# Block-diagonal state and one-chunk pipelining in linear attention, full-width stationary operands in a Fourier layer

## The chip, the cores and the metric

The kernel runs on one core of a Trainium2 chip. The metric is the device time of one execution in microseconds (us). Profile times below are counted from the first instruction of the profiled execution.

## The reference

Two layers follow each other. The first is linear attention with a decay per head: batch 4, 8 heads, 768 positions, head size 64. The second is a Fourier mixing layer on the joined heads (model size 512) with an MLP of inner size 2048. All data is fp32.

```python
for b in range(nb):                      # blocks of the sequence
    intra = (q_b @ k_b.T * Dmask) @ v_b  # Dmask = lam ** (i - j) for i >= j
    inter = (q_b * lam_pow) @ kv_state   # kv_state: 64 x 64 per head
    out[:, :, sl] = intra + inter
    kv_state = lam_block * kv_state + (k_b * rev_pow).T @ v_b
...
x = out.transpose(0, 2, 1, 3).reshape(B, S, H * D)
u = x + real(fft(fft(x, axis=1), axis=2))
un = (u - mean(u)) / sqrt(var(u) + 1e-06)
return u + relu(un @ w_ch1) @ w_ch2
```

The result does not depend on the block size, and the kernel uses chunks of 128 positions, so there are six chunks per batch.

## The kernel before

**Stages.** The program is written as Python generators that yield estimated costs; a hand-written weave (`beside`, `weave`, `part`, at the end of the kernel) takes turns between them, and a scheduler at build time may still move an instruction of an engine ahead of another unless it is pinned with `tc.keep_in_program_order`. Each engine then runs its own list strictly in order. The weave first runs attention of batch 0 beside the conversion of weights, then the Fourier layer of batch 0 beside attention of batch 1, then, from about 95 us on, the MLP of the first four groups of rows with everything else of the front end (attention and Fourier of batches 1 to 3) woven into it. From about 430 us on the MLP of the remaining rows runs alone (`late`), with products that the change does not touch.

**Attention, one chunk.** `attn_in` (L259) loads k, q and v on SP's queue (two buffers each), multiplies k by its decay on GpSimd (L270, tile kd, one buffer), transposes k and q on TensorE (L274, L279) and copies both out of PSUM on ScalarE (L276, L281). The 8 heads stand as 4 pairs: head 2p is on partitions 0 to 63 and head 2p+1 on 64 to 127 of pair p. From the transposed q VectorE also makes qs, q times its decay (L285). `attn_out` (L289) makes the scores (L298), one product per head with 64 rows and 128 columns of the array, masks them on VectorE (L302, tile sc), makes the state update (L315, 128 rows and 64 columns), and adds to the output in PSUM first the state product (L328, 64 rows and 64 columns, st times qs) and then the masked scores times v (L332, 128 rows and 64 columns). The state has two tiles that take turns: GpSimd multiplies the old one by the decay of a chunk (L319), VectorE adds the update (L320), and the state product of the chunk reads the old one. The output is copied by ScalarE (L335), transposed back (L348) and copied out (L352, L353). For batches other than 0, rows go to DRAM and are gathered back mirrored by GpSimd's queue (`mirror_a`, `mirror_b`, L439 to L452) for the Fourier layer.

In each group of eight products the two heads of a pair follow each other, so that the two halves of the array take turns. PSUM tiles of attention and Fourier layer share five buffers (`psum_a`).

**Fourier layer.** `fft_ln` (L491) folds rows with their mirror images on VectorE (`fold_x`, L426 to L484), transforms along the sequence with five products per batch, each of two output parts and two pieces of rows (L516), copies the results on ScalarE (L520), and transforms along the width (`width`, L524, matmuls L529 to L534). The fifth product of the sequence step needs one output row, and so does a last call of `width` (`only_a`, L607): both use a stationary operand of one column. Then `norm` (L542) takes mean and variance on VectorE, the root on GpSimd (L550, L551), and normalises (L564).

**Weights** come as 512 KB pieces on SP's queue (L209) and each is converted by two steps on ScalarE and five on VectorE (L216 to L225).

Of the kernel before, what the change touches and what calls it, by code (L numbers as in the profile page):

```python
# [10 lines left out]
F32 = mybir.dt.float32  # L11
# [65 lines left out]
def kernel(  # L77
# [95 lines left out]
    mhalf = const.tile([128, G], F32, name="mhalf")  # L173
    nc.gpsimd.memset(mhalf, -0.5)

    st = [const.tile([128, HP, D], F32, name=f"st{i}") for i in range(2)]


    cs = const.tile([128, 2, 2, 2, NK], F32, name="cs")
# [65 lines left out]

    def attn(b):

        head = () if b - 1 in LEADS else attn_in(b, 0)
        for c in range(NC):
            yield from head  # L250
            head = attn_in(b, c + 1) if c < NC - 1 else attn_in(b + 1, 0) if b in LEADS else ()
            yield from attn_out(b, c, head)

    ins, oTs, eo = {}, {}, {}
    LEADS = (0,)
# [3 lines left out]
    def attn_in(b, c):  # L259
        rows = slice(c * C, (c + 1) * C)  # L260
        kt, qt, vt = (new(ld, [C, H, D], nm) for nm in ("k", "q", "v"))
        for t, src in ((kt, k), (qt, q), (vt, v)):
            nc.sync.dma_start(t, src[b, :, rows, :].rearrange("h p d -> p h d"))
        if b == 0:
            load_tables(c)

        kd = None
        if c < NC - 1:
            kd = new(at, [C, H, D], "kd")
            nc.gpsimd.tensor_tensor(kd, kt, kpow, op=ALU.mult)  # L270

        ptk = psum_a([128, HP, C])
        for hp in range(HP):
            nc.tensor.transpose(ptk[:, hp, :], pair(kt, hp), ident)  # L274
        kT = new(at, [128, HP, C], "kT", bufs=2)
        nc.scalar.copy(kT, ptk)  # L276
        ptq = psum_a([128, HP, C])
        for hp in range(HP):
            nc.tensor.transpose(ptq[:, hp, :], pair(qt, hp), ident)  # L279
        qT = new(at, [128, HP, C], "qT", bufs=2)  # L280
        nc.scalar.copy(qT, ptq)  # L281
        qs = None
        if c > 0:
            qs = new(at, [128, HP, C], "qs")
            nc.vector.tensor_tensor(qs, ptq, qpow, op=ALU.mult)  # L285
        ins[b, c] = kT, qT, qs, kd, vt
        yield 1.2

    def attn_out(b, c, head):  # L289
        kT, qT, qs, kd, vt = ins.pop((b, c))  # L290
        last = c == NC - 1


        mm = nc.tensor.matmul
        pss = [psum_a([C, HP, C]) for _ in range(2)]
        for hp in range(HP):
            for hi in range(2):
                mm(pss[hi][:, hp, :], lhsT=kT[HD[hi], hp, :], rhs=qT[HD[hi], hp, :], start=True, stop=True)  # L298
        sc = []
        for hi in range(2):  # L300
            t = new(at, [C, HP, C], "sc", bufs=3)
            nc.vector.tensor_tensor(t, pss[hi], decay[:, hi::2, :], op=ALU.mult)  # L302
            sc.append(t)
        if last and b - 1 in LEADS:
            mirror_a(b, pin=True)
        yield 1.5


        s_old, s_new = st[(c + 1) % 2], st[c % 2]
        if not last:  # L310
            pu = psum_a([128, HP, D])
            for hp in range(HP):
                for hi in range(2):
                    h = 2 * hp + hi
                    mm(pu[HD[hi], hp, :], lhsT=kd[:, h, :], rhs=vt[:, h, :], start=True, stop=True)  # L315
            if c == 0:
                nc.vector.tensor_copy(s_new, pu)
            else:
                nc.gpsimd.tensor_tensor(s_new, s_old, spow.broadcast_to([128, HP, D]), op=ALU.mult)  # L319
                nc.vector.tensor_tensor(s_new, s_new, pu, op=ALU.add)  # L320
            yield 0.9


        po = psum_a([128, HP, C])
        if c > 0:
            for hp in range(HP):
                for hi in range(2):
                    mm(po[HD[hi], hp, :], lhsT=s_old[HD[hi], hp, :], rhs=qs[HD[hi], hp, :],  # L328
                       start=(hp == 0), stop=False, skip_group_check=True)
        for hp in range(HP):  # L330
            for hi in range(2):
                mm(po[HD[hi], hp, :], lhsT=vt[:, 2 * hp + hi, :], rhs=sc[hi][:, hp, :],  # L332
                   start=(c == 0 and hp == 0), stop=(hp == HP - 1), skip_group_check=True)
        oT = new(at, [128, HP, C], "oT")
        nc.scalar.copy(oT, po)  # L335
# [6 lines left out]
        yield 2.0  # L342
        yield from head

        def turn(oT):
            px = psum_a([C, HP, 128])
            for hp in range(HP):
                nc.tensor.transpose(px[:, hp, :], oT[:, hp, :], ident)  # L348
# [36 lines left out]

        px = turn(oTs[b]) if c > 1 else None
        if c > 0:

            oTs[b] = new(fp, [128, DM + 4], "ds")[:, 0:DM].rearrange("p (h c) -> p h c", h=HP)
            tc.keep_in_program_order(nc.scalar.copy(oTs[b][:, :, C - 1:0:-1], po[:, :, 1:C]))  # L390
        if last:
            tc.keep_in_program_order(nc.scalar.copy(oTs[b][:, :, 0:1], first))
        if c > 1:
            mirrored(c - 1, px)
            yield 1.4
        if not last:
# [94 lines left out]
    def fft_ln(b):  # L491
        sets = []

        def piece(a, i, n):

            c0 = W + QM if i == 4 else QM * (i % 2)
            return sets[a][i in (2, 3)][0:BLK[a], n, c0:c0 + (1 if i == 4 else QM)]

        if b in LEADS:
            yield from fold_a(b)  # L500
# [10 lines left out]
        for i in range(5):  # L511
            ps = psum_a([128, 2, NK])
            m = 128 if i < 4 else 1
            for n in range(2):
                for a, rows in enumerate(BLK):
                    mm = nc.tensor.matmul(ps[0:m, n, :], lhsT=piece(a, i, n), rhs=cs[0:rows, a, i in (2, 3), n, :],  # L516
                                          start=(a == 0), stop=(a == 1))
                    if i + n + a == 0:
                        tc.keep_in_program_order(mm)
            nc.scalar.copy(ys[i][0:m, 0:2 * NK].rearrange("p (k n) -> p n k", n=2), ps[0:m])  # L520
            yield 1.4


        def width(t, ps, only_a):  # L524
            y = [ys[i][:, 128 * t:min(128 * t + 128, S // 2 + 1)] for i in range(5)]
            ps = ps[0:1] if only_a else ps
            mm = nc.tensor.matmul
            if not only_a:
                mm(ps[:, HM + QM:DM], lhsT=y[2], rhs=dt[:, 2, 0:QM], start=True, stop=True)  # L529
# [651 lines left out]
    def run(gen):  # L1181
        return sum(gen)
# [20 lines left out]

    att1, mix = attn(1), fft_ln(0)
    att0 = attn(0)
    run(part(att0, 2.7))
    run(beside(att0, NC * t_chunk - 2.7, w, 0.25 * NW))

    run(beside(part(mix, T_FOLD), T_FOLD, att1, 3.25 * t_chunk))
# [55 lines left out]
```

## Time and profile before

| | us |
|---|---|
| median of 3 runs (799.5 to 799.83) | 799.71 |
| the profiled execution's own time | 799.14 |
| its span, first to last instruction | 797.2 |
| TensorE matmuls busy | 768.7 (96%) |
| VectorE busy | 586.4 (74%) |
| ScalarE busy | 217.3 (27%) |
| GpSimd busy | 196.5 (25%) |

The page's chain that ended last lies to 79% on TensorE. In lines of the profile, `128*64 128x128` behind a matmul is the part of the array that the stationary operand takes (rows*columns) and the operand that is streamed (partitions x elements). An fp32 product counts as two passes, so eight products are `x16`; a transpose counts as one. PEld is the load of the stationary operand. A busy matmul includes the end of its pipeline, so how long a group holds TensorE is read from the start of one group to the start of the next.

### The profile page before, as it was taken

How to read it: one execution, taken by the hardware profiler on the slowest of the kernel's cores; microseconds unless marked ns; L12 is line 12 of the kernel's file. 1: busy time of each engine (PE TensorE's matmuls, PEld its weight loads, DVE VectorE, ACT ScalarE, POOL GpSimd, SP SyncE). 2: the span in 40 equal slices, each digit the busy share in tenths (PEclk: the TensorE clock that was granted, in tenths of full speed). 3: DMA queues.
4: the chain of work that ended last, by engine and by line, in shares of the span. 5: the costliest groups of instructions: out<-in, count | busy, mean ns of one | idle time of the engine just before them, and what ended most of it. 6: DMA issues, size and time to landing. Idle time of an engine off the chain costs nothing.

```text
span 797.2 us, 14576 instructions
## 1 busy us (share of the span) xinstructions
PE 768.7 (96%) x5616; PEld 643.0 (81%) x5616; DVE 586.4 (74%) x1148; ACT 217.3 (27%) x512; POOL 196.5 (25%) x196
## 2 busy tenths in 40 slices
PE   6989999999999999999999999999999999999996
PEld 5767766758575766777855889998999999999996
DVE  6898889775844573246597998669977699758983
ACT  3755443224421211221200221012210342024300
POOL 3233340011111020121002960279304100230012
PEclk9999999999999999999999999999999999999998
DMA  9969623237842136443232365345854555455442
GB/s 252 253 148 271 181 84 121 81 75 202 215 122 83 40 66 141 101 136 107 49 67 83 145 234 168 103 159 193 318 176 145 163 183 175 131 173 183 135 120 80
DMA packets 152331, 116.80 MB, mean 147 GB/s; under 512 B 113998, under 2 KB 113998, under 8 KB 152262
## 3 DMA queue, kind: packets, MB, share of 16 engines
q1 hardware_dynamic: 147120, 103.39, 45.7%
q0 software_dynamic: 2112, 6.69, 2.6%
q10 hardware_dynamic: 3030, 5.78, 2.1%
q8 instruction: 45, 0.74, 0.4%
q14 instruction: 24, 0.20, 0.1%
HBM read 83.58 MB, written 32.25 MB: 145 GB/s over the span
## 4 chain that ended last, share of the span: by engine, by line
PE 79%; DVE 9%; DMA 4%; issue 4%; ACT 2%; POOL 1%; POOLq 0%; ACTq 0%; DVEq 0%
PE p L1038 21%; PE p L883 12%; PE p L968 11%; PE pm L650 10%; PE pm L636 8%; PE pa L332 3%; PE pa L516 3%; PE pa L298 3%; DMA x<-xb,ix 2%; PE pa L328 2%; PE pa L274 1%; PE pa L315 1%; DVE sc L302 1%; PE pa L279 1%; PE pa L348 1%
## 5 line engine op out<-in xcount | busy, mean ns | idle before, releaser
L636 PE MATMUL pm<-ut,w 128*128 128x256 f32 x512 | 119.2, 382 | 0.0
L650 PE MATMUL pm<-w,hr 128*128 128x512 f32 x256 | 116.1, 598 | 0.2 <-DVE w L225 0.2
L636 PEld LDWEIGHTS pm<-ut,w 128*128 128x128 f32 x512 | 94.4, 190 | 15.4 <-issue 3.6
L650 PEld LDWEIGHTS pm<-w,hr 128*128 128x128 f32 x256 | 46.9, 191 | 49.8 <-issue 48.2
L1052 POOL TENSOR_TENSOR y<-y,u 128x512 f32<-128x512 f32 x12 | 18.9, 1572 | 199.1 <-DVE y L1061 156.7
L1038 PE MATMUL p<-tx,sx 128*128 128x128 f32 x416 | 54.9, 275 | 0.0
L1038 PEld LDWEIGHTS p<-tx,sx 128*128 128x128 f32 x416 | 50.6, 192 | 0.0
L883 PE MATMUL p<-ur,w 128*128 128x256 f32 x192 | 46.9, 379 | 0.1
L270 POOL TENSOR_TENSOR kd<-k,decay 128x512 f32<-128x512 f32 x20 | 23.0, 1152 | 93.8 <-PE pa L315 60.7
L1046 DVE TENSOR_TENSOR y<-p,y 128x128 f32<-128x128 f32 x92 | 25.6, 286 | 22.4 <-PE p L1038 15.7
L1044 ACT COPY y<-p 128x128 f32<-128x128 f32 x48 | 12.8, 266 | 104.1 <-PE p L1038 103.8
L883 PEld LDWEIGHTS p<-ur,w 128*128 128x128 f32 x192 | 36.3, 190 | 5.7 <-issue 0.5
L302 DVE TENSOR_TENSOR sc<-pa,decay 128x512 f32<-128x512 f32 x48 | 31.5, 683 | 8.4 <-PE pa L298 8.2
L1038 PE MATMUL p<-w,ha 128*128 128x128 f32 x288 | 37.4, 275 | 0.0
L298 PEld LDWEIGHTS pa<-qT,kT 64*128 64x128 f32 x384 | 26.0, 193 | 13.1 <-ACT qT L281 7.2
L332 PE MATMUL pa<-sc,v 128*64 128x128 f32 x384 | 32.3, 286 | 3.5 <-DVE sc L302 3.5
L1038 PEld LDWEIGHTS p<-w,ha 128*128 128x128 f32 x288 | 35.0, 192 | 0.2
L644 ACT ACTIVATE hr<-pm 128x256 f32<-128x256 f32 x44 | 16.7, 385 | 67.5 <-PE pm L636 67.3
L550 POOL TENSOR_SCALAR ve<-mv 128x2 f32<-128x2 f32 x12 | 3.4, 287 | 123.3 <-DVE mv L547 123.3
L298 PE MATMUL pa<-qT,kT 64*128 64x128 f32 x384 | 30.7, 292 | 3.2 <-ACT qT L281 2.9
L883 PE MATMUL p<-sx,w1s 128*128 128x256 f32 x128 | 32.9, 380 | 0.2 <-DVE sx L786 0.2
L332 PEld LDWEIGHTS pa<-sc,v 128*64 128x64 f32 x384 | 23.6, 139 | 11.2 <-DVE sc L302 5.3
(227 smaller groups left out, 1709.0 us busy)
## 6 DMA issues: line engine op xcount, KB each, us to landing
tx<-td SPq DMA_DIRECT2D x84, 256.0 KB, 2.8
raw<-in_moe_w_ch_dram SPq DMA_DIRECT2D x32, 512.0 KB, 5.3
tx<-sd SPq DMA_DIRECT2D x42, 256.0 KB, 2.7
sd<-tx SPq DMA_DIRECT2D x28, 256.0 KB, 2.0
k<-in_k_dram SPq DMA_DIRECT2D x24, 256.0 KB, 5.0
q<-in_q_dram SPq DMA_DIRECT2D x24, 256.0 KB, 5.7
v<-in_v_dram SPq DMA_DIRECT2D x24, 256.0 KB, 4.8
td<-tx SPq DMA_DIRECT2D x21, 256.0 KB, 2.0
```

What stands on the lines that cost most here:

```text
L270: nc.gpsimd.tensor_tensor(kd, kt, kpow, op=ALU.mult)
L298: mm(pss[hi][:, hp, :], lhsT=kT[HD[hi], hp, :], rhs=qT[HD[hi], hp, :], start=True, stop=True)
L302: nc.vector.tensor_tensor(t, pss[hi], decay[:, hi::2, :], op=ALU.mult)
L332: mm(po[HD[hi], hp, :], lhsT=vt[:, 2 * hp + hi, :], rhs=sc[hi][:, hp, :], start=(c == 0 and hp == 0), stop=(hp == HP - 1), skip_group_chec ...
L516: mm = nc.tensor.matmul(ps[0:m, n, :], lhsT=piece(a, i, n), rhs=cs[0:rows, a, i in (2, 3), n, :], start=(a == 0), stop=(a == 1))
L636: nc.tensor.matmul(ps, lhsT=w1[:, c, 128 * fc:128 * fc + 128], rhs=ut[:, c, :], start=(c == 0), stop=(c == KO - 1))
L650: nc.tensor.matmul(ps, lhsT=hr[(fc - f0) // 4][:, fc % 4, 128 * i:128 * i + 128], rhs=w2[:, fc, :], start=(fc == f0), stop=(fc == f1 - 1))
L883: nc.tensor.matmul(ps, lhsT=s2.A[a][:, kt, 128 * i:128 * i + 128], rhs=U[b][:, kt, :], start=(first and kt == 0), stop=(kt == 1), skip_gro ...
L968: nc.tensor.matmul(ps[:, 128 * i:128 * i + 128], lhsT=ab[m][0][:, 128 * i:128 * i + 128], rhs=ab[m][1], start=(start and i == 0), stop=Tru ...
L1038: nc.tensor.matmul(ps[:, 0:HM // 2], lhsT=ab[m][0][i], rhs=ab[m][1][:, i, :], start=(start and i == 0), stop=(i == HF // 2 - 1), skip_grou ...
L1046: V.tensor_tensor(o, ps[:, 0:HM // 2], o, op=ADD)
L1052: nc.gpsimd.tensor_tensor(o, y, u, op=ADD)
```

## The change

The state becomes one tile of 128 partitions with, for each pair of heads, two blocks of 64 columns: block 0 holds head 2p on partitions 0 to 63 and zeros below, block 1 zeros and then head 2p+1. The tile is cleared once on GpSimd. The state product then uses all 128 rows of the array and 64 columns, as the output product and the state update do. The decay of a chunk (L318 of the new program) runs in place on the whole tile, and the add of the update (L324) runs once for each half of the partitions.

Attention is reordered: scores and mask of chunk c+1 (`attn_first`) are issued ahead of the state product of chunk c; qs of the next chunk is made after the state product, from the copied q in SBUF instead of PSUM; state product, output product and state update follow each other in this order, the first instruction of each pinned. Masked scores get four buffers for three, the transposed k one for two. `attn` starts the next chunk's input ahead of the transposes of the last chunk's output.

In the Fourier layer the fifth product of the sequence step takes 128 columns and writes 128 rows of PSUM, of which the copy still reads one; the last call of `width` streams against one column repeated 128 times.

```diff
-    st = [const.tile([128, HP, D], F32, name=f"st{i}") for i in range(2)]
+    st = const.tile([128, HP, 2, D], F32, name="st")
+    nc.gpsimd.memset(st, 0.0)
...
     def attn(b):
-        head = () if b - 1 in LEADS else attn_in(b, 0)
+        if b - 1 not in LEADS:
+            yield from attn_in(b, 0)
+            attn_first(b, 0)
+        back = ()
         for c in range(NC):
-            yield from head
-            head = attn_in(b, c + 1) if c < NC - 1 else attn_in(b + 1, 0) if b in LEADS else ()
-            yield from attn_out(b, c, head)
+            nxt = (b, c + 1) if c < NC - 1 else (b + 1, 0) if b in LEADS else None
+            if nxt:
+                yield from attn_in(*nxt)
+            yield from back
+            back = attn_out(b, c, nxt)
+            yield from part(back, 4.4)
+        yield from back
...
-        kT = new(at, [128, HP, C], "kT", bufs=2)
+        kT = new(at, [128, HP, C], "kT")
...
-        qs = None
-        if c > 0:
-            qs = new(at, [128, HP, C], "qs")
-            nc.vector.tensor_tensor(qs, ptq, qpow, op=ALU.mult)
-        ins[b, c] = kT, qT, qs, kd, vt
+        ins[b, c] = kT, qT, kd, vt
...
+    def attn_state(b, c):
+        kd, vt = ins[b, c][2:]
+        pu = psum_a([128, HP, D])
+        for hp in range(HP):
+            for hi in range(2):
+                h = 2 * hp + hi
+                mm = nc.tensor.matmul(pu[HD[hi], hp, :], lhsT=kd[:, h, :], rhs=vt[:, h, :], start=True, stop=True)
+                if h == 0:
+                    pin(mm)
+        if c > 0:
+            nc.gpsimd.tensor_tensor(st, st, spow.broadcast_to([128, HP, 2 * D]).rearrange("p h (a d) -> p h a d", a=2), op=ALU.mult)
+        for hi in range(2):
+            s = st[HD[hi], :, hi, :]
+            if c == 0:
+                nc.vector.tensor_copy(s, pu[HD[hi]])
+            else:
+                nc.vector.tensor_tensor(s, s, pu[HD[hi]], op=ALU.add)
...
+        if nxt:
+            if nxt[1]:
+                attn_first(*nxt)
         if last and b - 1 in LEADS:
             mirror_a(b, pin=True)
...
-                    mm(po[HD[hi], hp, :], lhsT=s_old[HD[hi], hp, :], rhs=qs[HD[hi], hp, :],
-                       start=(hp == 0), stop=False, skip_group_check=True)
+                    i = mm(po[HD[hi], hp, :], lhsT=st[:, hp, hi, :], rhs=qs[:, hp, :],
+                           start=(hp == 0), stop=False, skip_group_check=True)
+                    if hp + hi == 0:
+                        pin(i)
...
+        if not last:
+            attn_state(b, c)
+        if nxt and nxt[1] == 0:
+            attn_first(*nxt)
+        elif nxt:
+            qs = scores[(*nxt, 1)] = new(at, [128, HP, C], "qs")
+            nc.vector.tensor_tensor(qs, ins[nxt][1], qpow, op=ALU.mult)
...
-            return sets[a][i in (2, 3)][0:BLK[a], n, c0:c0 + (1 if i == 4 else QM)]
+            return sets[a][i in (2, 3)][0:BLK[a], n, c0:c0 + QM]
...
-                    mm = nc.tensor.matmul(ps[0:m, n, :], lhsT=piece(a, i, n), rhs=cs[0:rows, a, i in (2, 3), n, :],
+                    mm = nc.tensor.matmul(ps[:, n, :], lhsT=piece(a, i, n), rhs=cs[0:rows, a, i in (2, 3), n, :],
...
-            y = [ys[i][:, 128 * t:min(128 * t + 128, S // 2 + 1)] for i in range(5)]
-            ps = ps[0:1] if only_a else ps
+            y = [ys[i][:, S // 2:S // 2 + 1].broadcast_to([128, 128]) if only_a else ys[i][:, 128 * t:128 * t + 128] for i in range(5)]
...
-    run(part(att0, 2.7))
+    run(part(att0, 1.3))
```

`attn_first(b, c)` holds the scores and their mask as they stood in `attn_out` (L295 to L303), and keeps the masked scores in a table by chunk.

More of the change, by code (lines that the diff above doesn't have):

```diff
@@ L281, in attn_in, with attn_first @@
         nc.scalar.copy(qT, ptq)
-        qs = None
-        if c > 0:
-            qs = new(at, [128, HP, C], "qs")
-            nc.vector.tensor_tensor(qs, ptq, qpow, op=ALU.mult)
-        ins[b, c] = kT, qT, qs, kd, vt
+        ins[b, c] = kT, qT, kd, vt
         yield 1.2
[L289 to L294, printed above, removed]
+    scores, pin = {}, tc.keep_in_program_order
+    def attn_first(b, c):
+        kT, qT = ins[b, c][:2]
         pss = [psum_a([C, HP, C]) for _ in range(2)]
@@ L297, in attn_out @@
             for hi in range(2):
-                mm(pss[hi][:, hp, :], lhsT=kT[HD[hi], hp, :], rhs=qT[HD[hi], hp, :], start=True, stop=True)
-        sc = []
+                nc.tensor.matmul(pss[hi][:, hp, :], lhsT=kT[HD[hi], hp, :], rhs=qT[HD[hi], hp, :], start=True, stop=True)
+        sc = scores[b, c] = []
         for hi in range(2):
-            t = new(at, [C, HP, C], "sc", bufs=3)
+            t = new(at, [C, HP, C], "sc", bufs=4)
             nc.vector.tensor_tensor(t, pss[hi], decay[:, hi::2, :], op=ALU.mult)
@@ L304, in attn_out @@
+    def attn_out(b, c, nxt):
+        last = c == NC - 1
+        mm = nc.tensor.matmul
+        if nxt:
+            if nxt[1]:
+                attn_first(*nxt)
         if last and b - 1 in LEADS:
             mirror_a(b, pin=True)
[L306 to L311, printed above, removed]
+        sc, vt = scores.pop((b, c)), ins[b, c][3]
+        po = psum_a([128, HP, C])
+        if c > 0:
+            qs = scores.pop((b, c, 1))
@@ L312, in attn_out @@
             for hp in range(HP):
                 for hi in range(2):
[L314 to L328, printed above, removed]
-                       start=(hp == 0), stop=False, skip_group_check=True)
+                    i = mm(po[HD[hi], hp, :], lhsT=st[:, hp, hi, :], rhs=qs[:, hp, :],
+                           start=(hp == 0), stop=False, skip_group_check=True)
+                    if hp + hi == 0:
+                        pin(i)
         for hp in range(HP):
@@ L331, in attn_out @@
             for hi in range(2):
-                mm(po[HD[hi], hp, :], lhsT=vt[:, 2 * hp + hi, :], rhs=sc[hi][:, hp, :],
-                   start=(c == 0 and hp == 0), stop=(hp == HP - 1), skip_group_check=True)
+                i = mm(po[HD[hi], hp, :], lhsT=vt[:, 2 * hp + hi, :], rhs=sc[hi][:, hp, :],
+                       start=(c == 0 and hp == 0), stop=(hp == HP - 1), skip_group_check=True)
+                if hp + hi == 0:
+                    pin(i)
+        if not last:
+            attn_state(b, c)
@@ L341, in attn_out @@
                 nc.scalar.copy(oTs[b][:, :, 0:1], po[:, :, 0:1])
-        yield 2.0
-        yield from head
+        ins.pop((b, c))
+        yield 4.4
         def turn(oT):
```

## The prediction

> **What bounds the kernel now.** First the page's shares (96% TensorE), then the busy time stage by stage, then TensorE's waits, then the timeline of single groups. In the table by stretch the columns are start:end and length, then busy us and count of TensorE, its weight loads, VectorE, ScalarE and GpSimd, then TensorE clock, DMA share and GB/s.
>
> ```profile
> 0.00:50.00 50.00, 40.36 (x450) 32.26 (x450) 39.86 (x81) 29.95 (x66) 13.43 (x25) 1.00 0.95 236
> 50.00:100.00 50.00, 45.68 (x505) 38.06 (x504) 43.93 (x95) 24.13 (x55) 18.21 (x16) 1.00 0.78 205
> 126.00:210.00 84.00, 82.87 (x503) 59.23 (x502) 61.66 (x133) 33.49 (x72) 8.11 (x12) 1.00 0.55 145
> 210.00:265.00 55.00, 53.93 (x327) 35.98 (x326) 27.48 (x59) 12.71 (x27) 9.05 (x9) 1.00 0.38 103
> 300.00:366.00 66.00, 66.00 (x497) 46.76 (x496) 22.17 (x45) 12.72 (x30) 11.59 (x13) 1.00 0.56 139
> ```
>
> There are two regimes. From about 100 us, attention is woven into the MLP's products and TensorE is never free (66.00 of 66): any TensorE time removed there shortens the kernel. Before 100 us, attention of batches 0 and 1 stands with the conversion of weights and the Fourier step of batch 0; VectorE is 88% busy between 50 and 100 us, the DMA engines 95% before 50 us, and TensorE itself idles 14 us. Time saved on TensorE there may just become waiting.
>
> What TensorE waits for before 50 us, then between 50 and 100 us (total, times, longest):
>
> ```profile
> PE pa L274 <- DMA k<-in_k_dram: 4.8, 1, 4.8
> PE pa L298 <- ACT qT L281: 1.9, 4, 0.7
> PE pa L332 <- DVE sc L302: 1.1, 2, 1.0
> ```
> ```profile
> PE pa L348 <- ACT oT L335: 1.2, 1, 1.2
> PE pa L328 <- DVE qs L285: 0.8, 1, 0.8
> ```
>
> Short waits on the chain scores, mask, output. Now one chunk in the second regime (start, length, group; a product counts as two passes, so x16 is eight products):
>
> ```profile
> 203.18 2.74 PE L650 MATMUL pm<-w,hr 128*128 128x512 f32 x6
> 205.85 1.16 PE L298 MATMUL pa<-qT,kT 64*128 64x128 f32 x16
> 206.95 3.70 PE L650 MATMUL pm<-w,hr 128*128 128x512 f32 x8
> 210.58 0.69 PE L315 MATMUL pa<-v,kd 128*64 128x64 f32 x16
> 211.19 1.09 PE L328 MATMUL pa<-qs,st 64*64 64x128 f32 x16
> 212.21 1.09 PE L332 MATMUL pa<-sc,v 128*64 128x128 f32 x16
> 213.24 0.66 PE L274 MATMUL pa<-ident,k 128*128 128x128 f32 x4
> 213.73 0.60 PE L279 MATMUL pa<-ident,q 128*128 128x128 f32 x4
> ```
>
> Take distances from start to start. A dense 512-column pass takes 0.43 us (8 passes of L650 ahead of an untiled group take 3.43), so a 128-column pass 0.107. L298, L328 and L332 alternate between two halves of the array that run at once: 16 passes need 16 x 0.107 / 2 = 0.86 us, those of L315 (64 columns) 0.43. They take 1.10, 1.02, 1.03 and 0.61. So each group pays 0.16 to 0.24 us when its tiling ends, whoever follows. Entering costs too: the x6 group takes 2.67 where 2.58 is due (+0.09 into 64*128), the x8 group 3.63 where 3.43 is due (+0.2 into 128*64). The first transposes after a tiled group take 0.49, plain ones 0.44 (+0.05).
>
> [...] 1-column and 128-column products of the width step both take 0.22 us a pair. [...] the state's decay on GpSimd (L319), 0.62 at its shortest, once took 3.82 us.
>
> **The change, part by part.** I count in the order of TensorE's instructions, before and as the changed program is built, and split at the first MLP product (about 95 us).
>
> *Block-diagonal state, pinned groups.* The state product becomes 128*64 like the output product, and state product, output product and state update run as one group. Behind the split the order before has 34 runs of L315, L328 or L332 that end in another tiling, the new one 12: 22 x 0.17 = 3.7 us. Entries from untiled work into such a run fall from 14 to 2: 12 x 0.19 = 2.3. Returns to untiled work fall from 33 to 14: 19 x 0.05 = 0.9. Ahead of the split: ends 34 to 12 (3.7) and entries 5 to 2 (0.6). This presumes that state product to output product to update, one tiling but different operands, costs nothing between them. The trace does not show that junction; it lies between 0 and the 0.17 of an ended group. I take 0, because the width products change operands and lengths within one tiling at 0.22 a pair with nothing extra. The product itself keeps 128 streamed columns, so 0.86 us; zeros cost nothing more.
>
> *Alternation.* In four of the 24 score groups the old order puts two or three products on the same half in a row; they took 1.51 to 1.66 us where others take 1.10. In the new order all 24 alternate: 4 x 0.48 = 1.9 us, half of it behind the split.
>
> *Fourier products.* The fifth height product (one column) and the last width group (one column) are tilings of their own: behind the split seven runs at 0.09 in and 0.09 out, 7 x 0.18 = 1.3 us, one run (0.2) ahead. With 128 columns the products last as long as their neighbours (L516: 0.16 a pass either way), so nothing is added. More PSUM rows are written, but ScalarE still copies one.
>
> *Pipelining.* Scores and mask of chunk c+1 now precede the outputs of chunk c. That takes the mask (L302) off TensorE's path. In exchange, input transposes of chunk c+2 stand right behind the state update of chunk c. No instruction is added on TensorE.
>
> *Added on VectorE.* The state add is split by halves: two of about 0.41 (0.33 start to start) for one of 0.41, 20 chunks: 20 x 0.33 = 6.6 us, of which 10 x 0.33 = 3.3 ahead of the split. The scaled queries now read SBUF for PSUM, 0.68 either way[...]. Behind the split VectorE is 34 to 73% busy in the stretches shown, so its share hides there behind MLP products; without that cover it would be 3.3 us.
>
> *Added on GpSimd.* The decay covers 128x512 for 128x256: L270, the same size, takes 1.06, so +0.44 on 0.62, 16 times, 7 us on an engine busy 25%. It is issued before the next kd multiply (L270), waits for the state product and has finished about when the update group ends (1.3 us later), so it costs nothing unless blocked. The clearing of the state at the start (128x512, an estimate of 0.5 from the 0.42 of a 128x386 one) ends before k lands at 4.76: nothing.
>
> *Queues.* On SP the first two chunks' k, q and v now come ahead of tables and weights, so each weight is loaded about one place later and one fewer is converted before the first normalisation (-2.5 us of VectorE there). Every moved load keeps its two buffers. The pinned gather for batch 1 stands on GpSimd ahead of the first normalisation's root; three gathers at 1.0 to 1.2 each can hold that root back some 3 us.
>
> *Sum.* Behind the split 3.7 + 2.3 + 0.9 + 0.9 + 1.3 = 9.1. Two waits there should move by about a microsecond each way (an L516 wait of 1.23 near 370 gains MLP cover; chunks back to back near 330 to 350 may wait for k): net 0. Ahead of the split TensorE sheds 3.7 + 0.6 + 1.0 + 0.2 = 5.5, but VectorE sets the end: it idles some 11 us in waits between 8 and 100 us, takes on 3.3, sheds 2.5, and the root may be late. Bounds: -3 to +5.5; I take 1.5. What is late next there is VectorE's Fourier chain. Together 10.6: span 797.2 - 10.6 = 786.6. The profiled execution took 799.14 for a span of 797.2, so 1.9 lies outside: 788.5; the median of the runs is 0.6 above that execution: 789.1.
>
> **Rivals.** *Loads of k come late.* A buffer of k is free after the kd multiply of the chunk (1.06 behind the update group); k takes 5.0 us to land. It was then needed about two chunks later, now one: 1.1 + 0.4 issue + 5.0 = 6.5 us, against 5.7 for a back-to-back chunk of the new order. At 0.7 a chunk for some 11 such chunks 7.7 us are lost: 796.8. For it: DMA at 95% before 50 us. Against it: the loop covers two chunks, and TensorE waits for k once only now.
>
> [...] Then the junctions keep 0.17 each, some 38 in all, 6.3 lost: 795.4. For it: the junction isn't shown. Against it: the width products.
>
> *The state's chain takes over: slower.* The state product waits for decay and two adds of the chunk before; with it in a pinned group everything in TensorE's queue waits, MLP products too. Its cover shrinks from the 6 us of a chunk to 2.8 (transposes and scores between). If decay is blocked as at 72.50 (3.82 us) and the adds stand behind three weight steps (1.9 us on VectorE), the state is ready 2.5 + 1.9 + 0.8 = 5.2 us after the update, 2.4 late. It decides from 0.66 us a chunk over 16 chunks, the whole gain; at 1 us each 16 are lost: 794.5 if only a third are so, 805.1 if all. For it: VectorE at 88%. Against it: median decay is 0.67, and behind 210 us VectorE is half idle.
>
> **How the numbers follow.** Forecast 0.62 (its own times 784 to 793), late k 0.15[...], state chain 0.08, the rest, early stage better than bounded or the root's delay larger, 0.07. The range 784 to 797 takes in the sum with all 5.5 early microseconds and one wait gone, and both milder rivals. Faster by over 0.2% (what a measurement of this kernel can tell from no change: below 798.1) 0.88, within 0.04, slower 0.08.
>
> **What would show it.** Right: state product, output product and update start 0.86, 0.86 and 0.6 us apart, no score group over 1.2, no one-column group, fewer TensorE us between 126 and 366. Wrong: 1.02 still between state and output product; TensorE waiting for k or for the state in each early chunk; the first MLP product no earlier than now, or later.

## The result, and the profile after

The changed kernel takes 810.06 us (median of 7 runs, 807.67 to 810.61), the kernel before 799.83 in the same series: ratio 1.0111, 95% interval 1.0086 to 1.0135. It is slower, by 10.2 us between the medians, 8.9 by the ratio. The forecast was 789.1 (784 to 797).

The profiled execution took 810.3 us for a span of 808.4 (before: 799.14 and 797.2). First the same stretches of time as before, in the changed kernel (start:end and length, busy us and count of TensorE, its weight loads, VectorE, ScalarE and GpSimd, then TensorE clock, DMA share and GB/s):

```profile
0.00:50.00 50.00, 34.17 (x386) 29.76 (x388) 38.11 (x72) 24.32 (x51) 13.87 (x25) 0.90 0.85 213
50.00:100.00 50.00, 42.74 (x530) 38.48 (x526) 47.58 (x92) 25.47 (x62) 14.23 (x11) 0.97 0.72 180
100.00:126.00 26.00, 18.92 (x100) 16.51 (x101) 17.13 (x43) 8.96 (x24) 5.25 (x7) 0.87 0.31 97
...
300.00:366.00 66.00, 65.42 (x512) 46.92 (x511) 32.65 (x66) 13.21 (x29) 11.87 (x13) 1.00 0.49 107
```

Two things stand out. In the first 50 us TensorE is busy 34.17 us where it was 40.36, and part of that at a granted clock of 0.90 in the mean where it was 1.00. And VectorE is now busy 47.58 of the 50 us that follow, where it was 43.93. From 300 to 366 us TensorE is full in both kernels (65.42 and 66.00).

What TensorE waits for before 50 us, then from 50 to 100 us:

```profile
PE pa L282 <- DMA k<-in_k_dram: 7.6, 3, 5.0
PE pa L301 <- ACT qT L289: 3.8, 5, 1.0
PE pa L371 <- DVE st L324: 1.8, 1, 1.8
PE pa L287 <- DMA q<-in_q_dram: 1.2, 1, 1.2
```
```profile
PE pa L301 <- ACT qT L289: 2.9, 4, 1.4
PE pa L340 <- DVE qs L356: 1.4, 1, 1.4
```

Before, only the first k was waited for (4.8; it is the 5.0 of the 7.6 here). Now one chunk behind the split, to be laid beside the chunk shown of before (start, length, group):

```profile
344.57 1.16 PE L301 MATMUL pa<-qT,kT 64*128 64x128 f32 x16
345.66 1.09 PE L340 MATMUL pa<-qs,st 128*64 128x128 f32 x16
346.59 1.04 PE L346 MATMUL pa<-sc,v 128*64 128x128 f32 x16
347.46 0.64 PE L314 MATMUL pa<-v,kd 128*64 128x64 f32 x16
348.03 0.66 PE L282 MATMUL pa<-ident,k 128*128 128x128 f32 x4
```

Start to start: scores 1.09, state product 0.93 (was 1.02), output product 0.87 (was 1.03), update with its exit 0.57. The state product and the output product no longer pay an end of tiling, as forecast (0.93 and 0.87 for 1.02 and 1.03); the junction between them, and the zeros in the state, cost 0.07 at most (0.93 for the 0.86 due).

So where did the time go? The first MLP product starts at 110.57 us instead of 95.50: 15.1 us are lost ahead of the split. From there to the first product of the last stage it takes 330.3 us instead of 334.0: 3.7 us are won. Together 11.4, the difference of the spans (11.2) to within 0.2.

### The profile page after: what moved, and what is told of

The parts are those of the page before. It is cut to its first block, busy times and chain, and to the rows that moved or that the text cites. A ratio compares the mean times of both kernels' runs of the same rounds, so it can differ in the third digit from the quotient of the medians.

```text
span 808.4 us, 14623 instructions
## 1 busy us (share of the span) xinstructions
PE 759.5 (94%) x5616; PEld 650.7 (80%) x5616; DVE 606.5 (75%) x1168; ACT 217.3 (27%) x512; POOL 196.4 (24%) x197
## 4 chain that ended last, share of the span: by engine, by line
PE 71%; DVE 15%; issue 5%; DMA 3%; ACT 2%; POOL 2%; SPq 1%; POOLq 0%; ACTq 0%; DVEq 0%
PE p L1060 21%; PE p L905 12%; PE p L990 11%; PE pm L672 9%; PE pm L658 6%; PE pa L539 3%; PE pa L301 2%; PE pa L340 2%; PE pa L346 1%; DVE un L586 1%; DVE sc L305 1%; DVE stt L568 1%; DVE w L226 1%; POOL rs L573 1%; DMA x<-xb,ix 1%
## 5 line engine op out<-in xcount | busy, mean ns | idle before, releaser
L318 POOL TENSOR_TENSOR st<-st,qpow 128x512 f32<-128x512 f32 x16 | 19.6, 1226 | 109.3 <-PE pa L340 76.9
L664 DVE TENSOR_SCALAR hr<-pm 128x256 f32<-128x256 f32 x20 | 8.4, 418 | 32.5 <-PE pm L658 32.5
```

The costliest lines, as they stand in the source:

```text
L318: nc.gpsimd.tensor_tensor(st, st, spow.broadcast_to([128, HP, 2 * D]).rearrange("p h (a d) -> p h a d", a=2), op=ALU.mult)
```

## The experiments

The theory to begin with: the new order of attention, put among the loads and conversions of weights, loses the 15 us; behind the split the change does what it should. The rival: the block-diagonal state (larger decay on GpSimd, split adds) costs them. A table of all runs first. "First MLP" is the start of the first MLP product in the profiled execution, "rest" the span from there on. That mark scatters by some 2 us between executions of one kernel (105.65 and 107.66 in the two profiles of the kernel with spare products), so small differences in it are weighed with the times.

| run | first MLP | rest | median us | ratio to before (95%) |
|---|---|---|---|---|
| before | 95.50 | 701.7 | 799.83 | 1 |
| after | 110.57 | 697.8 | 810.06 | 1.0111 (1.0086 to 1.0135) |
| x1_old_front | 96.19 | 695.9 | 794.68 | 0.9947 (0.9929 to 0.9964) |
| x2_old_back | 109.69 | 703.5 | 815.54 | 1.0181 (1.0141 to 1.0221) |
| fourier_only | 95.65 | 702.2 | 799.14 | 0.9987 (0.9965 to 1.0009) |
| late_gather | 107.96 | 699.2 | 807.90 | 1.0095 (1.0075 to 1.0116) |
| block_old_order | 104.94 | 696.4 | 803.24 | 1.0038 (1.0024 to 1.0051) |
| new_order_64 | 105.78 | 699.7 | 807.53 | 1.0092 (1.0059 to 1.0125) |
| half_decay | 107.73 | 697.3 | 806.31 | 1.0076 (1.0046 to 1.0106) |
| one_add | 108.02 | 699.1 | 810.22 | 1.0139 (1.0111 to 1.0167) |
| kd_two_buffers | 105.21 | 698.2 | 807.15 | 1.0094 (1.0071 to 1.0117) |
| three_mended | 102.14 | 699.0 | 804.47 | 1.0047 (1.0023 to 1.0070) |
| noconv_new, noconv_old | 106.38, 95.90 | 698.3, 699.0 | 806.56, 796.99 | one run each |
| mended_no_weights, old_no_weights | 92.94, 93.22 | 698.9, 701.6 | 793.85, 796.61 | one run each |
| spare_products | 105.65 | 699.1 | 807.02 | one run |
| spare_timed | 107.66 | 698.9 | 808.89 | 1.0109 (1.0066 to 1.0152) |

**Old front, old back.** The old attention stands beside the new one in the program, and the batch chooses:

```diff
+    OLD = (0, 1)          # x2_old_back: (2, 3)
     def attn(b):
+        if b in OLD:
+            ... the loop, the two state tiles and the outputs of before
+            return
```

> Batches 0 and 1 keep the order and the two state tiles of before (as halves of the new tile), batches 2 and 3 have the new order and the block-diagonal state; the Fourier change stays. If the loss sits in attention of batches 0 and 1, ahead of the first MLP product, and the gain behind it is real: that product starts near 95 us as before, and the time is 799.8 - 7 to 9 = 791 to 793. If the new order costs time in every batch, or the gain behind 148 us was only the pay-back of work that had been displaced: 798 to 810.

> The other half: batches 0 and 1 have the new order and the block-diagonal state, batches 2 and 3 those of before; the Fourier change stays. If the loss sits in batches 0 and 1: first MLP product near 110 us as after, and 810.1 + 6 to 8 = 816 to 818. If the loss is shared by all batches: 803 to 808.

Measured 794.68 and 815.54; first MLP product at 96.19 and 109.69. The two add up: -5 and +16 against the kernel before make the +10 of the whole change, to within 1. The loss sits in batches 0 and 1, whole. x1_old_front beats both kernels (0.9947); its gain, 5 us, is less than the 7 to 9 expected.

**Fourier part alone.** Edit: the three lines of the diff in `piece`, the height products and `width`.

> Only the Fourier products get 128 stationary columns; attention as before. Forecast of the sum: 7 runs at 0.18 behind the split are 1.3 us, so 798.5, with 0.2 more if the one ahead counts. Rival, the narrow products cost no change of tiling: 799.8, no change. Rival, it is part of the loss: over 801.

Measured 0.9987 with an interval that holds 1. It isn't part of the loss; 0.5 us is all that the time shows of the 1.3. The trace shows where the rest went: from the first MLP product to the first product of the last stage TensorE is busy 325.5 us instead of 327.1, but waits 8.6 instead of 6.9.

**Block state in the old order, old state in the new order.**

```diff
 block_old_order (the order of before)
-    st = [const.tile([128, HP, D], F32, name=f"st{i}") for i in range(2)]
+    st = [const.tile([128, HP, 2, D], F32, name=f"st{i}") for i in range(2)]
...
-                    mm(po[HD[hi], hp, :], lhsT=s_old[HD[hi], hp, :], rhs=qs[HD[hi], hp, :],
+                    mm(po[HD[hi], hp, :], lhsT=s_old[:, hp, hi, :], rhs=qs[:, hp, :],
 new_order_64 (the changed kernel)
-                    i = mm(po[HD[hi], hp, :], lhsT=st[:, hp, hi, :], rhs=qs[:, hp, :],
+                    i = mm(po[HD[hi], hp, :], lhsT=st[HD[hi], hp, :], rhs=qs[HD[hi], hp, :],
```

> The order of before, with block-diagonal state products (two tiles of 128x512 that take turns, decay on the whole tile, add by halves, one buffer for the transposed k) and the Fourier change. If the loss ahead of the MLP comes from the order: the first MLP product stays near 95 us, and update, state product and output product, which stand together there, gain behind it: 799.1 - 4 to 8 = 791 to 795. If it comes from the larger decay on GpSimd and the split adds: first product after 103 us, time over 803.

> The changed kernel with the state of before in one tile: 64-row state products, decay on 128x256, one add. If the loss comes from the order: first MLP product still at 107 us or later, and the state product is a tiling of its own again, 24 or so switches at 0.2 to 0.4 more: 811 to 816. If the larger decay and the split adds cause it: first product near 97 us, 798 to 802.

Here my theory fell. The block-diagonal state in the old order makes the first MLP product 9 us late, and the kernel slower than before (1.0038) although its rest is 5.3 us shorter. The old state in the new order still has it 10 us late. Both parts lose, each by itself; that 9 and 10 don't add up to the 15 of the two together says that they share some of it. (The single buffer for the transposed k isn't it: the batches of the old order in x1_old_front have it too.)

How each part loses is read from the whole stretch up to the first MLP product (columns as above; the third pair is VectorE). In order: fourier_only, block_old_order, new_order_64, the changed kernel:

```profile
0.00:95.65 95.65, 81.74 (x933) 67.29 (x934) 81.61 (x167) 53.08 (x118) 27.86 (x38) 1.00 0.87 217
0.00:104.94 104.94, 84.24 (x933) 68.86 (x934) 90.90 (x177) 53.66 (x118) 31.14 (x41) 0.98 0.79 196
0.00:105.78 105.78, 81.24 (x933) 69.78 (x933) 82.06 (x162) 51.59 (x114) 27.81 (x39) 0.93 0.80 204
0.00:110.57 110.57, 81.42 (x933) 72.15 (x934) 89.53 (x172) 51.35 (x114) 32.41 (x40) 0.91 0.77 195
```

With the block-diagonal state in the old order VectorE works 9.3 us longer (90.90 for 81.61) and idles as long as without it (14.0 us in both): that is the whole delay. With the new order and the old state it works 0.5 us longer and idles 9.7 us longer. The changed kernel has both, 7.9 us of work and 7.0 of waits. So the state loses through VectorE's work, the order through waits. (That the sums agree more closely than the mark's scatter of 2 us is luck.)

Of the 9.3 us, 16 adds of the state by halves (6.6 us) stand for 8 whole ones (3.3), and four copies of the first update (1.7) for two (0.8): 4.2. The five conversion steps of 13 weight pieces take 39.2 us instead of 37.0 with nothing changed in them: 2.2. The remainder is spread over other instructions. Some of the longer steps stand beside a GpSimd instruction. In the changed kernel a conversion step beside a decay on GpSimd, and the same step later without one:

```profile
32.15 1.57 POOL L318 TENSOR_TENSOR st<-st,qpow 128x512 f32<-128x512 f32 x1 [8.76 <-PE pa L340]
32.73 1.27 DVE L218 TENSOR_SCALAR e<-raw 128x512 uint16<-128x512 uint16 x1
37.79 0.42 DVE L218 TENSOR_SCALAR e<-raw 128x512 uint16<-128x512 uint16 x1
```

A step beside a kd multiply (33.92) takes 1.28 us likewise. The new order has a cost of this kind too: qs, which now reads two SBUF tiles, takes 896 ns in the mean in the front of the changed kernel and 1541 at the longest, where the one that read PSUM took 683 and 692 in the kernel before: 2.1 us over ten. The three longest (1.54, 1.37 and 1.23 us at 22.39, 83.53 and 95.15) start while GpSimd runs a kd multiply or a decay; the shortest took 0.68. To split the two causes that the state brings, larger decay and split adds, in the changed kernel:

```diff
 half_decay
-            nc.gpsimd.tensor_tensor(st, st, spow.broadcast_to([128, HP, 2 * D]).rearrange("p h (a d) -> p h a d", a=2), op=ALU.mult)
+            nc.gpsimd.tensor_tensor(st[:, :, 0, :], st[:, :, 0, :], spow.broadcast_to([128, HP, D]), op=ALU.mult)
 one_add
-        for hi in range(2):
-            s = st[HD[hi], :, hi, :]
+        s = st[:, :, 0, :]
...
-                nc.vector.tensor_tensor(s, s, pu[HD[hi]], op=ALU.add)
+            nc.vector.tensor_tensor(s, s, pu, op=ALU.add)
```

> The changed kernel with GpSimd's decay on block 0 of each pair only (128x256, as large as before): the odd heads' state isn't decayed. If the larger decay[...] is what the block-diagonal state costs ahead of the MLP: first MLP product at 106 to 107 us, 807 to 808. If the split add is: 810.

> The changed kernel with one VectorE add (0.41 us) of the whole update into block 0 of each pair instead of two adds by halves (0.84): the odd heads' update lands in the wrong block. If the split add is what the block-diagonal state costs ahead of the MLP: first MLP product at 106 to 107 us, 807 to 808. If the decay on GpSimd is: 810.

In the time, one add for two changes nothing (810.22, 1.0139), and half the decay gives 806.31 (1.0076). The interval of half_decay overlaps that of the changed kernel (1.0111), but not that of one_add. In the profiles the two look alike: VectorE works 86.00 us up to the mark with half the decay and 85.66 with one add, instead of 89.53, and both marks (107.73 and 108.02) come 2.5 to 2.8 us earlier. So both parts load VectorE, and how the delay is shared between them isn't settled.

The conversion steps don't settle it either. All five on 12 pieces take 36.6 us in the changed kernel, 33.6 with half the decay and 37.0 with one add, as if the decay did it; but they take 36.9 in three_mended, whose decay is small, and 33.9 in spare_products, whose decay is large (both below). It would fit if the number of steps that fall beside a GpSimd instruction changed from kernel to kernel; that was not shown.

**Gathers behind the root.**

```diff
-        if last and b - 1 in LEADS:
-            mirror_a(b, pin=True)
...
             elif last:
+                if b - 1 in LEADS:
+                    mirror_a(b, pin=True)
                 mirror_b(b)
```

> The changed kernel, with the three gathers of batch 1 issued on GpSimd behind the first normalisation's root instead of ahead of it; nothing else moves on TensorE, VectorE or ScalarE. If the gathers hold the root back by what its wait shows (3.3 us on VectorE): first product of the MLP near 107 instead of 110.6, and 810.1 - 3 to 4 = 806 to 807. If the root is late for another reason, or the MLP's first products then wait for something else: 810.

GpSimd and VectorE at the first normalisation, in the changed kernel and in late_gather (start, length, in brackets the wait and what ended it):

```profile
100.53 1.45 POOL L462 DMA_INDIRECT fo<-xa,ix  x1 [4.69 <-ACT oT L358]
102.06 0.30 DVE L569 BATCH_NORM_AGGREGATE mv<-stt 128x2 f32<-128x6 f32 x2
102.28 0.94 POOL L462 DMA_INDIRECT fo<-xa,ix  x1 [0.31 <-issue]
103.53 0.97 POOL L468 DMA_INDIRECT x<-xa,ix  x1 [0.31 <-issue]
104.88 0.73 POOL L573 TENSOR_TENSOR rs<-ve,mhalf 128x2 f32<-128x2 f32 x1
105.64 0.74 DVE L586 TENSOR_SCALAR un<-x,mv,rs 128x256 f32<-128x256 f32 x2 [3.28 <-POOL rs L573]
```
```profile
101.96 0.73 POOL L573 TENSOR_TENSOR rs<-ve,mhalf 128x2 f32<-128x2 f32 x1
102.72 0.74 DVE L586 TENSOR_SCALAR un<-x,mv,rs 128x256 f32<-128x256 f32 x2 [1.16 <-POOL rs L573]
```

The variance is ready at 102.3, and the root has two gathers ahead of it. With the gathers behind it, VectorE waits 1.16 for the root instead of 3.28: 2.1 us. In the kernel before, these gathers come behind the root (92.75 and 90.18 us). The median is 2.2 lower, short of the 3 to 4 expected, and the two intervals overlap.

**Two buffers for the decayed k.** In the changed kernel the chain of one late k is this (update of a chunk, kd multiply, load, transposes):

```profile
14.35 0.64 PE L314 MATMUL pa<-v,kd 128*64 128x64 f32 x16
...
15.13 1.31 POOL L278 TENSOR_TENSOR kd<-k,decay 128x512 f32<-128x512 f32 x1 [7.00 <-PE pa L314]
...
16.56 0.38 SPq L271 DMA_DIRECT2D k<-in_k_dram  x1
...
23.33 0.63 PE L282 MATMUL pa<-ident,k 128*128 128x128 f32 x4 [1.28 <-DMA k<-in_k_dram]
```

The multiply waits for the update, because kd has one buffer; at 16.44 it is done and the k buffer is free; at 16.56 the load is issued; 6.8 us later k is there. The update of the next chunk had ended at 22.0. It is the rival of late k with its own numbers. The second buffer's room comes from leaving out the table of query factors:

```diff
-    qpow = const.tile([128, HP, C], F32, name="qpow")
-    for hp in range(HP):
-        scan(qpow[:, hp, :], lamq[:, hp:hp + 1].broadcast_to([128, C]), ident, 1.0, op0=ALU.mult, op1=ALU.bypass)
+    qpow = decay[:, 0:HP, :]
...
-            kd = new(at, [C, H, D], "kd")
+            kd = new(at, [C, H, D], "kd", bufs=2)
```

> The changed kernel with two buffers for the decayed k, so that the multiply needn't wait for the update of the chunk before and the k buffer comes free earlier. The room for it comes from the table of query factors, in whose place a slice of the mask's table is used (the state's and the queries' decay factors are thereby not the reference's; shapes and work are the same). If the three waits for k and q behind the first chunk (3.7 us) and the half clock that follows them come from the k buffer: they vanish, the granted clock at 25 to 35 us is 1.0, the last output product of batch 0 falls from 54.6 us to 48 to 51, the time from 810.1 to 804 to 807. If the loads are late because the queue and the DMA engines are full: no change, 809 to 811.

The work is not quite the same: the four scans (2.2 us on VectorE) are gone, here and in the two runs below that use this edit. They fell into a wait: VectorE's first mask still stands behind the first scores and starts at 9.84 us, at 10.06 in the changed kernel.

The last output product of batch 0 starts at 50.05 (54.60), the waits for k behind the first fall from 2.6 to 0.9 us, that for q stays at 1.2, and the granted clock of the first 50 us is 0.97 for 0.90. The time is 807.15, between the two expectations, with an interval that overlaps that of the changed kernel. So the buffer is a part of the late k in the trace; its share of the time isn't told apart.

**All three together.** Edit: new_order_64, late_gather and the second kd buffer in one kernel.

> The new order with three things put back or mended together: the state of before (64 rows, one tile, 128x256 decay, one add), two buffers for the decayed k (room as in the run with two buffers, with the same wrong factors), and the three gathers of batch 1 behind the root. If these are the whole loss ahead of the MLP: first MLP product at 95 to 98 us instead of 110.6 and the time near 799 - 3 = 796 (the tiling gain of the grouped order without that of the state product). If the new order loses by itself, whatever its buffers: first product at 101 or later, 801 to 805.

1.0047 is clearly under 1.0111: the three are 5 us of the time, and 8.4 of the 15.1 in the mark. But the first MLP product still comes at 102.14 and the kernel is still slower than before. 6.5 us are left with the new order. VectorE's work up to the mark is that of fourier_only by now (81.99 and 81.61 us); its waits are 6.1 us longer.

**Weights out of the way.** First without conversion of the first eight pieces, loads kept; then without loads too:

```diff
 noconv_new, noconv_old
+        if conv[0] <= 8:
+            nc.scalar.activation(dst, raw.bitcast(U16)[:, 3:4 * WP:4].bitcast(I16), AF.Sign)
+            return
 mended_no_weights, old_no_weights
+        if conv[0] <= 8:
+            nc.gpsimd.memset(dst, 0.5)
+            return
         nc.sync.dma_start(raw, src.bitcast(U32))
```

> The changed kernel, with the conversion of the first eight weight pieces left out: each is still loaded, and one ScalarE step writes a stand-in, in place of two ScalarE and five VectorE steps. Only the time of the front is read. If attention of batch 0 is late because kT and qT copies on ScalarE and masks on VectorE queue behind conversion steps: the last output product of batch 0 falls from 54.6 us to 46 to 49. If the new order itself is too short of TensorE work between update and next scores, whatever VectorE does: 52 or later.

> The same left out in the kernel with the order of before (with the Fourier change). If conversion steps are what sets the two orders apart: the last output product of batch 0 stays near 46 us or gains 1 to 3 us, and the distance to the new order without conversion is under 3 us. If they are not: the distance stays at about 8 us.

> The new order with the three things mended, and the first eight weight pieces neither loaded nor converted (a constant is written in their place on GpSimd, ahead of the second chunk's work). Only the front is read. If the 6.5 us left come from the supply of k and q beside the weights and from queues full of conversion steps: waits for k and q behind the first chunk near 0, first MLP product within 2 us of that of the old order without these weights. If the new order has too little TensorE work between the update and the next scores: k and q waits near 0 too, but the distance stays at 5 to 7 us.

> The order of before with the Fourier change and the same eight weight pieces left out. Old order: TensorE was busy 40 of the first 50 us and there waits 4.7 us for the first k and 4.6 us else, so 1 to 4 us are to be gained: first MLP product at 92 to 95 us.

Without conversions the last output products of batch 0 end at 51.5 instead of 55.7 us in the new order, and at 45.3 instead of 47.9 in the old: a distance of 6.2 for 7.8, so conversions alone don't set the two apart. The first MLP products stay 10.5 us apart. Without the loads as well, and with the three things mended, the new order has its first MLP product at 92.94 beside 93.22 in the old (one profile each), and its one run is 2.8 us shorter. TensorE's waits for loads before 50 us, in three_mended and then in mended_no_weights:

```profile
PE pa L282 <- DMA k<-in_k_dram: 8.6, 5, 4.7
```
```profile
PE pa L286 <- DMA k<-in_k_dram: 5.1, 1, 5.1
```

3.9 us for k and 0.9 for q behind the first chunk become nothing. With these weights gone the new order isn't behind: the 6.5 us that it loses by itself come from standing beside them. The loads, which make its k and q late, are the likelier part, since leaving out conversions alone did little. But how the 6.5 us divide is not told apart, since loads and conversions were left out together.

**Spare products.** TensorE's stretches of 5 us show where the granted clock falls in the changed kernel:

```profile
25.00:30.00 5.00, 3.81 (x24) 3.35 (x24) 3.37 (x7) 3.27 (x7) 0.00 (x0) 0.50 1.07 286
...
105.00:110.00 5.00, 3.28 (x15) 2.91 (x15) 1.47 (x4) 1.17 (x2) 0.61 (x1) 0.50 0.46 154
```

Both come behind waits. Between 22.1 and 25.1 us TensorE ran only the four transposes of k (0.63 us) between waits of 1.3 and 1.2, and the transposes of q behind them already take 1.08 us instead of 0.60, the scores 2.08 instead of 1.16. At 106, behind a wait of 5.1, the groups take two thirds longer (width products 0.64 for 0.39). To test whether the clock follows from the idle stretches:

```diff
+    def warm(b, c):
+        if b == 0 and c > 1:
+            mm = nc.tensor.matmul(psum_m([128, 512]), lhsT=ident, rhs=qpow.rearrange("p h c -> p (h c)"), start=True, stop=True)
+            tc.keep_in_program_order(mm)
...
+        warm(b, c)
         ptk = psum_a([128, HP, C])
...
         kT, qT = ins[b, c][:2]
+        warm(b, c)
```

> The changed kernel with one spare product (128 columns by 512, 0.86 us at full clock, its result unused) ahead of the k transposes and one ahead of the scores, from the third chunk of batch 0 on: eight of them, 6.9 us. If the half clock at 25 to 35 and 45 to 50 us follows from TensorE's idle stretches: granted clock 1.0 in the first 50 us, no score group over 1.2 us, and the last output product of batch 0 about where it was (54.6 us, between 52 and 56), since the spare products take from the waits and give back the clock. If the clock has another cause: it stays at 0.90 and that product comes at 56 to 61 us.

> The changed kernel with the eight spare products (6.9 us of extra work on TensorE in batch 0), now timed. If idle stretches cost a second time through the clock: 806 to 808, faster than the changed kernel without them by 2 to 4 us although it does more. If the profile's gain was scatter: 810 to 813.

The first run (807.02) had the clock at 1.00 for the first 50 us and the last output product of batch 0 at 51.05 us; the timed one has them at 1.00 and 52.52, against 0.90 and 54.60. The scores and the state product of one chunk in the timed one:

```profile
28.24 1.16 PE L308 MATMUL pa<-qT,kT 64*128 64x128 f32 x16 [1.61 <-ACT qT L295]
29.34 1.09 PE L347 MATMUL pa<-qs,st 128*64 128x128 f32 x16
```

The wait for qT is still there, even longer; the scores behind it take 1.16 and not 2.08. So in batch 0 the clock does follow from the idle stretches (1.00 with products put into them, 0.90 without), and with eight products more, 6.9 us of work, batch 0 is done 2 to 3.5 us earlier. In the time nothing of it can be told: 1.0109 beside 1.0111, and 808.89 lies between the two expectations. The clock's part in the lateness of batch 0 is shown; its share of the time lost stays unmeasured.

## Why the prediction was wrong, step by step

- *Behind the split, tilings, alternation and one-column products: 9.1 us.* Right. From the first MLP product to the first product of the last stage TensorE's time without waits falls from 327.1 (334.0 less 6.9 of waits) to 318.3 us (330.3 less 12.0): 8.8. In x1_old_front, with the front of before, it is 317.8: 9.3. Of it new_order_64 lacks 2.3 (331.4 less 10.9 is 320.5), and fourier_only alone has 1.6 where 1.3 was forecast.
- *State product, output product and update cost nothing between them.* Right: 0.93, 0.87 and 0.57. The rival in which each junction keeps 0.17 (chance 0.08) fell.
- *"Net 0" for the waits behind the split.* Wrong by 5.1 us. TensorE's longest waits there, in the changed kernel:

```profile
PE pa L591 <- DVE un L586: 3.0, 3, 1.0
PE pm L658 <- DVE hr L664: 1.6, 1, 1.6
...
PE pa L314 <- DVE sc L305: 1.2, 1, 1.2
PE pm L672 <- DVE w L226: 1.1, 1, 1.1
```

  Those for un were 2.6 before. New are MLP products that wait for their own relu on VectorE (1.6 and 0.5) and chunk groups that wait for masks to give back PSUM buffers. x1_old_front has 10.9 us of waits in this stretch too, so they come from the changed program behind the split (1.7 of the 5.1 stand in fourier_only too) and not from a late front. The prediction hid VectorE's additions behind MLP products without asking for whom VectorE then is late.
- *Ahead of the split: "Bounds: -3 to +5.5; I take 1.5".* This is the step that failed: -15.1. The bounds let VectorE take on 3.3 us and shed 2.5, 0.8 net. Measured up to the mark, it works 9.2 us longer (89.53 for 80.33), though it sheds its piece of weights as forecast, and idles 5.9 us longer. Not in the bounds, or too small in them:
  - *"Every moved load keeps its two buffers"*: true, but the rival of late k, with chance 0.15, came about in batch 0, at 7 us between updates, through the kd tile's single buffer and loads that land in 6.8 us and not 5.0. The prediction gave it 0.7 a chunk for eleven chunks; it showed as two waits of 1.3 for k and one of 1.2 for q, and behind the last two of these the granted clock fell to 0.50 (25 to 30 us).
  - *The decay "costs nothing unless blocked"*: it took up to 2.65 us for 1.05, and VectorE's steps beside it take longer too (1.27 us for 0.42). With the split adds and copies of the state (4.2 where 3.3 was forecast) and the longer steps, the state alone makes VectorE work 9.3 us longer in block_old_order and its first MLP product 9 us late. How much of that is the decay isn't settled.
  - *Scaled queries "0.68 either way"*: that is their shortest. They take 0.90 in the mean, up to 1.54 beside GpSimd, 2.1 us more in all.
  - *The root held back "some 3 us"*: 2.1, and what filled TensorE while the norm ran before, the last chunk's groups, was done by then: TensorE stood for 5.1 us, and its granted clock was 0.50 afterwards (105 to 110 us).
  - *Supply*: with the three mended, 6.5 us are left; without eight weight pieces they are gone. The sum had no term for an order that needs its inputs one chunk sooner in the stage where loads and conversions are densest.
- *The state's chain, the rival on the slower side*, was not what happened: only 0.3 us of waits of the state product for st are in the list of 50 to 100 us, none in that of the first 50 (the 1.8 of L371 there is a PSUM buffer that the add gives back). The kernel is slower through late inputs and VectorE's work, not through a state that isn't ready.

## What to carry to other kernels

A reordering is won or lost stage by stage: here the same change saves 9 us of TensorE work behind the first MLP product, and loses 15 ahead of it, where it stands among loads and conversions (DMA engines 0.85 busy in the first 50 us, VectorE 47.58 of the 50 that follow); with the old order and state kept there the kernel is 5 us faster (0.9947). When a step moves to an earlier need, follow its input back to the buffer that has to come free, past every single-buffered tile on the way, and time that chain with the landing of this stage (6.8 us here, where 5.0 was counted). And when an instruction on GpSimd grows, or one on VectorE reads SBUF instead of PSUM, look in the trace at what each takes beside the other, not only at whether each has time: here 1.27 us for 0.42, and up to 1.54 for 0.68.

## What the runs showed of the hardware

- Behind two waits of 1.3 and 1.2 us with 0.63 us of transposes between them the granted clock fell to 0.50 (25 to 30 us); the scores then took 2.08 us for 1.16, the transposes 1.08 for 0.60.
- 6.9 us of useless products put into the waits of batch 0 cost no time that can be measured (808.89 beside 810.06), and the granted clock of the first 50 us was 1.00 with them, 0.90 without.
- Single VectorE steps of 0.42 us, with one SBUF input, took 1.27 and 1.28 us beside a decay and a multiply on GpSimd; a product of two SBUF tiles took up to 1.54 us (0.68 at its shortest), the same product with one input in PSUM never over 0.69.
- Two groups of products in one tiling with different operands follow each other at 0.93 and 0.87 us, where a change of tiling in between made it 1.02 and 1.03.
